# A gated mix of attention and a long convolution on one core: which operand of the convolution is turned into Toeplitz tiles

## The chip, the cores and the metric

The kernel runs on one core of a Trainium2 chip. The metric is the device time of one execution in microseconds. Engines are named as in the profile: PE (TensorE matmul), PEld (its weight load), DVE (VectorE), ACT (ScalarE), POOL (GpSimd), SP (SyncE, which issues most DMAs).

## The reference

Two branches read a 2048 x 448 bfloat16 input `x` and are mixed row by row with a gate `g = sigmoid(sum(x * gate_w))`:

```
q = x @ wq (16 heads of 28), k = x @ wk, v = x @ wv      # one k and one v for all heads
a = softmax(q k^T / sqrt(28)) v, heads joined, @ wo
K[d, l] = Re sum_n C[d,n] * dt[d]*B[d,n] * exp(dt[d]*A[d,n] * l)    # d < 448, n < 256, l < 2048
b[:, d] = causal convolution of x[:, d] with K[d, :]  +  x[:, d] * Dskip[d]
out = g * a + (1 - g) * b
```

The convolution is per channel: 448 channels, each with its own 2048 taps.

## The kernel before, in words

**One program, ordered by a planner.** The kernel first describes every piece of work as an operation with an engine, an estimated duration, what it reads and writes, and a priority. A list scheduler (`Prog.schedule`) turns this into one fixed order per engine. Each engine then runs its order strictly from front to back, waiting on semaphores where an operand comes from elsewhere. So an instruction that waits holds up everything behind it on its engine. The planner gives each DMA a fixed latency (2.2 us and an `extra`), and for some readers it adds a slack (`slk`): the first matmul on a freshly loaded convolution tile is planned 2.5 us later than its operand is expected.

**Attention** sets the pace. There are 1024 score tiles of 128 keys x 512 queries (16 groups of 4 heads x 512 queries, 64 tiles each). They are taken in sets of three and two alternately, 410 sets. For each set PE writes scores to PSUM (`psS`, line 1181), ACT takes the exponential (`expT`, line 1205), and PE multiplies by the values, accumulating in the one bank `psB` (line 1214). `psS` holds two sets; `expT` is a ring of 15 tiles. At the end of each group of 64 tiles `psB` is copied to `acc` (line 1074, by ACT for groups 0 to 13), and the next group may write `psB` only after this copy. Then a chain of three POOL DMAs turns the sums into reciprocals on all partitions (`denT`, `R_scratch`, `rdenB`). In gaps of PE the planner inserts matmuls on zeros (lines 640 and 1187), which keep PE's activity up.

**The convolution** is woven into the same orders in 14 chunks `c` of 32 channels. For each chunk:

- DVE builds tables of powers (`tables`, lines 895 to 935), from masters built for 2 to 4 chunks at a time (`masters`, lines 856 to 874).
- `kgen`: PE multiplies the tables (line 959), DVE adds `Dskip` to tap 0 (line 969), ACT copies the taps to SBUF (line 972), and POOL writes them with nine DMAs to the scratch `KP` in DRAM.
- `tload`: SP loads a Toeplitz tile for each 4 channels out of `KP`. Partition p of the tile reads the same rows shifted by one element, so that one tile is 128 partitions x 4288 elements, 1072 KB. 112 tiles are loaded, into five slots of `T` and two more that come free late.
- `conv` (two per chunk): PE multiplies the tiles by `U` (the input, loaded once in blocks of 64 rows in a reversed order, shape 128 x 32 blocks x 448 channels), line 1015; DVE multiplies by 1 - g (line 1026), PE turns the result (line 1037), and DVE adds it to `O` (line 1045).

Chunk 13 is made in two halves (`HALVES`). At the end `outp` and `tail` project the attention with `Wo` and store `O`.

Of the kernel before, what the change touches and what calls it, by code (L numbers as in the profile page):

```python
# [6 lines left out]
ALU = mybir.AluOpType  # L7
# [4 lines left out]
P = 128  # L12
# [19 lines left out]
HALVES = (13,)  # L32
NTR = 5
# [47 lines left out]
class Prog:  # L81
# [52 lines left out]
    def dma(self, pairs, desc, slot, rd=(), wr=(), pr=0, eng="sp", slow=False, extra=0):  # L134
# [5 lines left out]
        o = self.op(eng, fn, nd * (30.0 + 0.03 * size if size < 1500 else 105.0 + 0.022 * size) / 16.0 * 1.1, rd, wr, pr)  # L140
# [5 lines left out]
        return o  # L146

    def schedule(self):
# [20 lines left out]
        while done < n:  # L169
# [55 lines left out]
            if o.slot is not None:  # L225
                free[e] = r + (1000.0 if e == "pool" else 500.0) * o.ndma
                s = r if e == "pool" else max(r, dmafree)
                end = s + o.ns + self.DMA_NS + o.extra
                dmafree = max(dmafree, s) + o.ns
            else:  # L230
                free[e] = r + o.ns
                end = free[e] + o.lat
# [124 lines left out]
class Kernel:  # L357
# [34 lines left out]
    def alloc(self):  # L392
# [23 lines left out]
        self.U = sb("U", D * 32, BF)  # L416
        self.O = sb("O", 16 * D, BF)
        self.T = sb("T", NTR * TW, BF)
        self.tslots = [(self.T, s * TW, ["tpdone", "rawdone"]) for s in range(NTR)]
        self.tslots.append((self.xT, NT * S - TW - 2048, [("xT", hp, q) for hp in range(2) for q in range(3)]))  # L420
        self.tmap, self.tlast = {}, [s - 9 for s in range(NTR)] + [-20, -20]
# [14 lines left out]
        self.cst = sb("cst", 512, BF)  # L436
# [4 lines left out]
        self.KP = nc.dram_tensor("KP_scratch", (2 * KH,), BF).ap()  # L441
# [4 lines left out]
    def consts(self):  # L446
# [6 lines left out]
        dm(V(self.kstg, 0, 256), 0.0, 170, [("kst", 0, 0), ("kst", 1, 0)])  # L453
# [10 lines left out]
        for k in range(2):  # L464
            dm(V(self.U, (16 + 8 * k) * D, 8 * D), 0.0, 1550, ["Uz"])
# [17 lines left out]
        dm(V(self.Wo, 0, NT * D), 0.0, 810, ["Wo"], 5)  # L483
        for q in range(4):
            dm(V(self.O, q * 4 * D, 4 * D), 0.0, 800, [("O", q)], 5)

    def loads(self):
# [14 lines left out]
        self.dtb = self.cst  # L502
# [21 lines left out]
        rs = self.U.rs  # L524
        for k, (h, p0, b0) in enumerate(((1, 16, 15), (0, 0, 15), (1, 0, 31))):
            ap = bass.AP(tensor=self.U.h, offset=h * rs + p0 * D, ap=[[2 * rs, 64], [D, 16], [1, D]])
            pg.dma([(ap, dram(x, 64 * b0 * D, [[D, 64], [-64 * D, 16], [1, D]]))],
                   (1024, 896), f"u{k}", rd=["Uz"] if p0 else [], wr=[("U", k)], pr=0.5)
        for k in range(2, 6):
# [6 lines left out]
        pg.dma([(dram(self.KP, KH + 1024, [[4 * KW, 112], [KW, 4], [1, 64]]), self.kstg.v(0, 112, 0, [[64, 4], [1, 64]]))],  # L536
               (448, 128), "pad", rd=[("kst", 0, 0), ("kst", 1, 0)], wr=["pad"], pr=3)
# [15 lines left out]
    def prep_x(self):  # L553
# [3 lines left out]
        for q in range(4):  # L557
# [43 lines left out]
            pg.op("pe", mv, 900, rd=["Wv", "Wvg"] + self.xk(q), wr=[("b", 6)], pr=0.5)  # L601
        pg.op("dve", lambda e: e.tensor_reduce(sm.v(0, P, 12, [[1, 1]]), sm.v(0, P, 8, [[1, 4]]), AX.X, ALU.max),
# [86 lines left out]
    def prep_gate(self):  # L689
# [11 lines left out]
        def mm(e):  # L701
            for mu in range(2):
                for par in range(2):
                    r = e.matmul(px.v(0, P, 64 * mu, [[1, 64]]), self.sel.v(0, 16, 128 * (1 + (1 - mu) - par), [[1, P]]),
# [126 lines left out]
    def masters(self, b):  # L831
# [22 lines left out]
        for k in range(11):  # L854
            if k:
                dv(lambda e, k=k: e.tensor_tensor(two(msq), both(k - 1), both(k - 1), ALU.mult), 2 * w, keys(k - 1), ["msq"])  # L856
                dv(lambda e, k=k: e.scalar_tensor_tensor(src(k, 1), src(k - 1, 0), 2.0, src(k - 1, 1), ALU.mult, ALU.mult),
# [13 lines left out]
        for lv in range(5):  # L871
            if lv:
                dv(lambda e: e.tensor_tensor(qq, qq, qq, ALU.mult), w, ["sqq"], ["sqq"])
# [64 lines left out]
    def kgen(self, c, sub=None):  # L938
# [13 lines left out]
        for jj in range(8):  # L952
            def mm(e, comp, jj=jj):
                for half in range(2):
                    for g in gs:
# [7 lines left out]
                            start=(comp == 0 and half == 0), stop=(comp == 1 and half == 1),  # L963
                            tile_position=(0, 32 * g), skip_group_check=True)
                return r
            for comp in range(2):
                pg.op("pe", lambda e, mm=mm, comp=comp: mm(e, comp), 226 if whole else 113, mode="c", st=2.08 if whole else 1.04,
                      rd=keys, wr=[X] + k1 + k2, pr=1.7, lock=G if jj == 0 and comp == 0 else None)
        pg.op("dve", lambda e: e.tensor_tensor(ko.v(p0, np, ks + 63, [[64, 8]]), G.v(p0, np, 63, [[64, 8]]),
                                               self.skt.v(p0, np, 8 * c, [[1, 8]]), ALU.add),  # L970
              el(8), rd=[X, "skt"], wr=k1, pr=2)
        pg.op("act", lambda e: e.activation(ko.v(p0, np, ks, [[64, 8], [1, 63]]), G.v(p0, np, 0, [[64, 8], [1, 63]]), AF.Copy),  # L972
              490, rd=[X] + k1, wr=k2, pr=-1, unlock=G)
        rs = ko.rs
        lst = [(dram(self.KP, (32 * c + 8 * gs[0]) * KW + 1024, [[8 * KW, len(gs)], [KW, 8], [1, 64]]),
                bass.AP(tensor=ko.h, offset=(p0 + 16) * rs + ks, ap=[[32 * rs, len(gs)], [64, 8], [1, 64]]))]
        for g in gs:
            for h in range(2):
                lst.append((dram(self.KP, h * KH + (32 * c + 8 * g) * KW, [[64, 16], [KW, 8], [1, 64]]),
                            ko.v(32 * g + 16 * h, 16, ks, [[64, 8], [1, 64]])))  # L980
        pg.dma(lst, (264 * len(gs), 128), f"kw{sub or 0}", rd=k1 + k2, wr=[("KP", 2 * c + h) for h in ((0, 1) if whole else (sub,))],
               pr=0, eng="pool", extra=2000)
# [8 lines left out]
    def tload(self, gi):  # L991
# [4 lines left out]
        pg.dma([(t.v(0, P, o, [[1, TW]]),  # L996
                 dram(self.KP, 4 * gi * KW, [[1, 64], [KH, 2], [1, TW]]))],
               (128, 2 * TW), f"T{s}", rd=[("KP", gi // 4), "pad"] + x, wr=[("T", s)] + y, pr=1, extra=2500)

    def conv(self, c):  # L1000
# [3 lines left out]
        ck, cx = ("cst", c % 2), [("xT", hp, 0) for hp in range(2)] if c == 1 else []  # L1004
# [295 lines left out]
```

## Time and profile before

| | |
|---|---|
| median of 3 runs | 537.56 us (537.3 to 541.54) |
| the profiled execution's own time | 540.75 us |
| its span in the profile | 539.0 us |
| mean granted PE clock | 0.965 |
| PE busy | 486.4 us (90%) |
| DVE busy | 449.5 us (83%) |
| ACT busy | 497.5 us (92%) |
| POOL busy | 102.1 us (19%) |
| DMA | 142.89 MB, 265 GB/s on average |

Durations below come from the one profiled execution, which is 3.2 us above the median of the three runs. A group's row gives its busy time, the mean duration of one instruction, and the idle time of the engine just before it with what ended it. Durations overlap a little with the next instruction's, so where it matters the distance from start to start is used.

### The profile page before, as it was taken

The page shows a single profiled execution, that of the slowest core. Times are in us where ns is not written, and L with a number is a line of the kernel's source. Part 1 is how long each engine was busy: PE and PEld are TensorE (multiplying, and loading weights), DVE is VectorE, ACT ScalarE, POOL GpSimd, SP SyncE. Part 2 cuts the span into 40 slices and gives each one's busy share as a digit, 9 for nine tenths or more (in the row PEclk, how much of TensorE's full clock was granted, in tenths as well). Part 3 has the DMA queues.
Part 4 walks back from the last instruction along what each step waited for, and adds up shares of the span by engine and source line. Part 5 has one row for each costly group of instructions (what it writes and reads, how often), then busy time and mean ns, then how long its engine had stood idle before and what let it go on. Part 6 is the DMA issues. An engine that isn't in the chain of part 4 may idle for free.

```text
span 539.0 us, 20180 instructions
## 1 busy us (share of the span) xinstructions
PE 486.4 (90%) x9186; PEld 249.5 (46%) x9186; DVE 449.5 (83%) x891; ACT 497.5 (92%) x458; POOL 102.1 (19%) x192
## 2 busy tenths in 40 slices
PE   7698999989999899888999898989999898999887
PEld 4442233235454555353555454553556355644434
DVE  7979999989999999899999999999999695331203
ACT  3799999998999999989999999999999796899992
POOL 2000002200431404012040430040042213220000
PEclk9989999998999999999999999999999796899998
DMA  8931100793398987979778989999859997999722
GB/s 235 283 121 47 37 21 7 251 347 116 118 376 300 329 358 284 351 259 386 296 240 363 327 273 348 400 351 367 343 191 356 353 380 287 348 344 392 261 88 71
DMA packets 39042, 142.89 MB, mean 265 GB/s; under 512 B 11240, under 2 KB 22032, under 8 KB 24620
## 3 DMA queue, kind: packets, MB, share of 16 engines
q1 hardware_dynamic: 28316, 135.30, 69.0%
q0 software_dynamic: 9104, 6.13, 4.4%
q8 instruction: 72, 1.18, 0.9%
q10 hardware_dynamic: 1536, 0.17, 0.3%
q14 instruction: 14, 0.11, 0.1%
HBM read 135.39 MB, written 5.74 MB: 262 GB/s over the span
## 4 chain that ended last, share of the span: by engine, by line
ACT 56%; PE 26%; DMA 8%; DVE 8%; issue 2%; ACTq 0%
ACT expT L1205 54%; PE psS L1181 7%; PE psB L1214 4%; PE psS L959 3%; PE psX L959 3%; DMA rdenB<-R_scratch 3%; PE psX L1015 3%; DMA denT<-acc 2%; DMA sz<-in_A_wv_dram 2%; PE psS L1015 2%; ACT acc L1074 1%; DMA R_scratch<-denT 1%; DVE msq L856 1%; DVE xT L576 1%; DVE tab L911 1%
## 5 line engine op out<-in xcount | busy, mean ns | idle before, releaser
L1205 ACT ACTIVATE expT<-psS 128x1536 bf16<-128x1536 f32 (+1 forms) x410 | 470.6, 1340 | 18.7 <-PE psS L1181 11.7
L1181 PE MATMUL psS<-qT,kT 32*128 32x512 bf16 x1024 | 164.3, 395 | 29.8 <-ACT expT L1205 22.3
L1214 PE MATMUL psB<-expT,vaug 128*32 128x512 bf16 x1024 | 105.1, 400 | 3.7 <-issue 3.2
L1181 PEld LDWEIGHTS psS<-qT,kT 32*128 32x128 bf16 x1024 | 39.5, 91 | 119.3 <-ACT expT L1205 97.3
L1187 PE MATMUL psB<-ident,zero 32*128 32x512 bf16 x190 | 74.9, 394 | 0.0
L911 DVE TENSOR_TENSOR tab<-tab,mbf 128x256 bf16<-128x256 bf16 (+5 forms) x75 | 69.6, 928 | 1.2
L1015 PE MATMUL psX<-T,U 128*18 128x128 bf16 (+7 forms) x1920 | 54.7, 243 | 4.2 <-issue 3.2
L1214 PEld LDWEIGHTS psB<-expT,vaug 128*32 128x32 bf16 x1024 | 26.4, 93 | 64.8 <-issue 62.8
L1015 PEld LDWEIGHTS psX<-T,U 128*18 128x18 bf16 (+7 forms) x1920 | 47.6, 161 | 15.1 <-issue 11.2
L640 PE MATMUL psB<-ident,zero 128*32 128x512 bf16 (+3 forms) x728 | 48.6, 336 | 0.0
L138 POOL DMA_DIRECT2D KP_scratch<-xT x64 | 34.4, 544 | 43.6 <-ACT xT L972 43.6
L138 POOL DMA_DIRECT2D KP_scratch<-kstg x63 | 34.1, 549 | 34.2 <-ACT kstg L972 32.5
L959 PE MATMUL psX<-tab 128*32 128x64 bf16 x960 | 39.7, 293 | 0.3 <-DVE tab L935 0.3
L913 DVE TENSOR_TENSOR tmp<-tab,mbf 128x256 bf16<-128x256 bf16 (+4 forms) x62 | 39.6, 638 | 0.0
L1015 PE MATMUL psS<-T,U 128*32 128x128 bf16 (+7 forms) x1344 | 39.3, 243 | 0.0
L138 POOL DMA_DIRECT2D denT<-acc x15 | 10.8, 717 | 146.8 <-ACT acc L1074 137.9
L1015 PEld LDWEIGHTS psS<-T,U 128*32 128x32 bf16 (+7 forms) x1344 | 34.0, 161 | 8.9 <-issue 6.9
L959 PE MATMUL psS<-tab 128*32 128x64 bf16 x832 | 35.3, 293 | 0.0
L138 POOL DMA_DIRECT2D R_scratch<-denT x15 | 8.6, 576 | 138.7 <-DVE denT L1082 59.2
L930 DVE TENSOR_TENSOR tab<-tab,tmp 128x2048 bf16<-128x2048 bf16 x28 | 33.5, 1219 | 0.2
L959 PEld LDWEIGHTS psX<-tab 128*32 128x32 bf16 x960 | 30.3, 138 | 6.7 <-issue 3.8
L959 PEld LDWEIGHTS psS<-tab 128*32 128x32 bf16 x832 | 26.4, 137 | 7.4 <-issue 5.4
(179 smaller groups left out, 599.1 us busy)
## 6 DMA issues: line engine op xcount, KB each, us to landing
T<-KP_scratch SPq DMA_DIRECT2D x102, 1072.0 KB, 11.0
xT<-KP_scratch SPq DMA_DIRECT2D x7, 1072.0 KB, 10.5
rdenB<-R_scratch POOLq DMA_DIRECT2D x15, 256.0 KB, 12.4
tab<-KP_scratch SPq DMA_DIRECT2D x3, 1072.0 KB, 8.8
U<-in_A_x_dram SPq DMA_DIRECT2D x3, 896.0 KB, 15.4
tab<-in_A_x_dram SPq DMA_DIRECT2D x4, 448.0 KB, 7.5
SZ_scratch<-tab SPq DMA_DIRECT2D x1, 1344.0 KB, 8.6
out_dram<-O SPq DMA_DIRECT2D x3, 448.0 KB, 3.8
```

The source lines that it names most:

```text
L138: return [e.dma_start(o, i, **kw) for o, i in pairs]
L576: pg.op("dve", lambda e, d=dst, s=src: e.tensor_copy(d, s), 1130, rd=[("b", b)], wr=[key], pr=-0.6)
L640: r = e.matmul(t.v(32 * j, 32, bo, [[1, 128 * m]]), self.zero.v(0, P, 0, [[1, 32]]), self.ident.v(0, P, 0, [[0, m], [1, P]]), start=not ac ...
L911: vo(lambda e, dst=dst, src=src, mr=mr: e.tensor_tensor(dst, src, mr, ALU.mult), 2 * n, done + mk(lv), kr + ki)
L913: vo(lambda e, src=src, mi=mi, w=w, n=n, tb=tb, to=to: e.tensor_tensor(tb.v(0, P, to, [[n, 2], [cw, w], [1, cw]]), src, mi, ALU.mult), 2 * ...
L930: vo(lambda e, h=h: e.tensor_tensor(tab.v(0, P, FM + 32 * h, [[64, 2], [EW, 32], [1, 32]]), tab.v(0, P, lo + 31 * EW + 64 * h, [[BLK, 2], ...
L959: r = e.matmul(G.v(32 * g, 32, 64 * jj, [[1, 64]]), tab.v(0, P, lo + comp * BLK + 32 + o, [[EW, 32]]), tab.v(0, P, fo, [[mo - fo, 2], [EW, ...
L1015: r = e.matmul(ps.v(32 * j, 32 - 2 * n, 128 * k, [[1, 128]]), self.U.v(0, P, 2 * n * D + 4 * gi + j, [[D, 32 - 2 * n]]), tb.v(0, P, to + j ...
L1181: r = e.matmul(self.psS.v(0, P, 512 * (bo + k), [[1, 512]]), kT.v(32 * h, 32, 128 * kt, [[1, 128]]), qT.v(32 * h, 32, 512 * (i % 2), [[1, ...
L1187: r = e.matmul(self.psB.v(0, P, 0, [[1, 512]]), self.zero.v(32 * h, 32, 0, [[1, P]]), self.ident.v(32 * h, 32, 0, [[0, 4], [1, P]]), start ...
L1205: pg.op("act", lambda e: e.activation(expT.v(0, P, 512 * es, [[1, n]]), self.psS.v(0, P, 512 * bo, [[1, n]]), AF.Exp, scale=SQ), 50 + n / ...
L1214: r = e.matmul(self.psB.v(32 * h, 32, 0, [[1, 512]]), vaug.v(0, P, 32 * kt, [[1, 32]]), expT.v(0, P, 512 * (t % RING), [[1, 512]]), start= ...
```

## The change

The roles of input and taps in the convolution are exchanged.

- The Toeplitz tiles are now made of x. The transposed input `xT` is stored to a scratch `XP` in four DMAs, with a pad of zeros, and `tload` reads from there. A tile no longer depends on `kgen`. At most three tile loads are in flight (`tops`); `T` has seven slots instead of five.
- The other operand, now `Ku`, holds the taps of one chunk in two buffers. `kgen` gets them there from the ACT copy with a transposing DMA from SBUF to SBUF (`X`, issued by SP) and four POOL DMAs (from `X` to `Ku`), two of them of 64 runs of 1 KB and two of 1024 runs of 32 bytes. `U` and its three loads are gone.
- `Dskip` is added by PE: four small matmuls at the end of `kgen` instead of the DVE addition. The ACT copy moves 512 columns in one piece.
- The copies of `psB` to `acc` in groups 0 to 13 move from ACT to DVE.
- `Wo`, `Ku` and `O` are cleared by DMAs from the tile of zeros. DVE's memsets of `Wo`, `O` and `U` are gone.
- `masters` writes its last level (k = 10, lv = 4) directly in bfloat16 without a copy after it. Chunk 13 is made in one piece.
- The planner's costs for DMAs are other ones, so that all orders change. The result of the convolution comes out unreversed, and the gate's table is laid out to match.

The core of the diff:

```diff
-HALVES = (13,)
-NTR = 5
+HALVES = ()
+NTR = 7
...
-        o = self.op(eng, fn, nd * (30.0 + 0.03 * size if size < 1500 else 105.0 + 0.022 * size) / 16.0 * 1.1, rd, wr, pr)
+        o = self.op(eng, fn, nd * (12.0 + 0.036 * size if size < 1500 else 105.0 + 0.022 * size) / 16.0 * 1.1, rd, wr, pr)
...
+    def tdma(self, out, inp, slot, rd, wr, pr):
+        o = self.dma([(out, inp)], (128, 1024), slot, rd, wr, pr, extra=1500)
+        o.fn = lambda e: [e.dma_start_transpose(out, inp)]
...
-                free[e] = r + (1000.0 if e == "pool" else 500.0) * o.ndma
+                free[e] = r + (550.0 if e == "pool" else 250.0) * o.ndma
...
-        self.U = sb("U", D * 32, BF)
+        self.Ku = sb("Ku", 2 * 1024, BF)
+        self.X = sb("X", 2 * 512, BF)
...
-        for k in range(2):
-            dm(V(self.U, (16 + 8 * k) * D, 8 * D), 0.0, 1550, ["Uz"])
...
-        dm(V(self.Wo, 0, NT * D), 0.0, 810, ["Wo"], 5)
-        for q in range(4):
-            dm(V(self.O, q * 4 * D, 4 * D), 0.0, 800, [("O", q)], 5)
+        for k, (b, n, keys, pr) in enumerate(((self.Wo, 14, ["Wo"], 1.9), (self.Ku, 16, [("Ku", 0, 0), ("Ku", 0, 1), ("Ku", 1, 0), ("Ku", 1, 1)], 4),
+                                              (self.O, 56, [("O", q) for q in range(4)], 5))):
+            pg.dma([(b.v(0, P, 0, [[P, n], [1, P]]), self.zero.v(0, P, 0, [[0, n], [1, P]]))], (P * n, 256), f"z{k}", rd=["zero"], wr=keys, pr=pr)
...
+            lst = [(dram(self.XP, (q // 2) * KH + 64 + 512 * (q % 2), [[KW, DT], [DT * KW, 4], [1, 512]]),
+                    xT.v(0, DT, 2048 * q, [[512, 4], [1, 512]]))]
+            if q == 1:
+                lst.append((dram(self.XP, KH, [[KW, DT], [DT * KW, 4], [1, 64]]), xT.v(0, DT, 2048 + 448, [[512, 4], [1, 64]])))
+            pg.dma(lst, (448, 1024), "xp", rd=self.xk(q), wr=[("XP", q)], pr=0.6)
...
-        pg.op("dve", lambda e: e.tensor_tensor(ko.v(p0, np, ks + 63, [[64, 8]]), G.v(p0, np, 63, [[64, 8]]),
-                                               self.skt.v(p0, np, 8 * c, [[1, 8]]), ALU.add),
-              el(8), rd=[X, "skt"], wr=k1, pr=2)
-        pg.op("act", lambda e: e.activation(ko.v(p0, np, ks, [[64, 8], [1, 63]]), G.v(p0, np, 0, [[64, 8], [1, 63]]), AF.Copy),
-              490, rd=[X] + k1, wr=k2, pr=-1, unlock=G)
-        rs = ko.rs
-        lst = [(dram(self.KP, (32 * c + 8 * gs[0]) * KW + 1024, [[8 * KW, len(gs)], [KW, 8], [1, 64]]),
-                bass.AP(tensor=ko.h, offset=(p0 + 16) * rs + ks, ap=[[32 * rs, len(gs)], [64, 8], [1, 64]]))]
-        for g in gs:
-            for h in range(2):
-                lst.append((dram(self.KP, h * KH + (32 * c + 8 * g) * KW, [[64, 16], [KW, 8], [1, 64]]),
-                            ko.v(32 * g + 16 * h, 16, ks, [[64, 8], [1, 64]])))
+        def tap(e):
+            for g in gs:
+                r = e.matmul(G.v(32 * g, 32, 63, [[64, 8]]), self.ident.v(0, P, 32 * g, [[1, 32]]), self.skt.v(0, P, 8 * c, [[1, 8]]),
+                             start=False, stop=True, tile_position=(0, 32 * g), skip_group_check=True)
+            return r
+        pg.op("pe", tap, 113 if whole else 57, mode="c", st=0.7 if whole else 0.35, rd=["skt", "id"], wr=[X], pr=1.6)
+        pg.op("act", lambda e: e.activation(ko.v(p0, np, ks, [[1, 512]]), G.v(p0, np, 0, [[1, 512]]), AF.Copy),
+              490, rd=[X], wr=k1 + k2, pr=-1, unlock=G)
...
+        pg.tdma(self.X.v(0, P, xo + r0, [[128, 4], [1, n]]), ko.v(p0, np, ks, [[1, 512]]), f"kt{sub or 0}", rd=k1 + k2,
+                wr=xk + (["dt"] if c < 1 else []), pr=0)
+        lst = []
+        for par in range(2):
+            for h, m, w in ((0, 0, 32), (1, 16, 16)):
+                dims = [[128, 4], [1, n]] if not h else [[32, 16], [1, w]] if whole else [[128, 4], [1, w]]
+                for r in (r0,) if whole or not h else (r0, r0 + 32):
+                    lst.append((bass.AP(tensor=self.Ku.h, offset=h * rs + uo + 512 * par + r, ap=[[2 * rs, 64]] + dims),
+                                bass.AP(tensor=self.X.h, offset=64 * par * xs + xo + r + m, ap=[[xs, 64]] + dims)))
+        pg.dma(lst, (1152, 64), f"kw{sub or 0}", rd=xk, wr=[("Ku", c % 2, h) for h in hs], pr=0, eng="pool", extra=1500)
...
-        pg.dma([(t.v(0, P, o, [[1, TW]]),
-                 dram(self.KP, 4 * gi * KW, [[1, 64], [KH, 2], [1, TW]]))],
-               (128, 2 * TW), f"T{s}", rd=[("KP", gi // 4), "pad"] + x, wr=[("T", s)] + y, pr=1, extra=2500)
+        pg.dma([(t.v(0, P, o, [[1, TW]]), dram(self.XP, 4 * gi * KW + 1, [[1, 64], [KH, 2], [1, TW]]))],
+               (128, 2 * TW), f"T{s}", rd=[("XP", q) for q in range(4)] + ["pad"] + x, wr=[("T", s)] + y, pr=1, extra=1500)
+        o = pg.ops[-1]
+        self.tops.append(o.i)
+        if len(self.tops) > 3:
+            o.deps[self.tops[-4]] = 1
...
-                                     self.U.v(0, P, 2 * n * D + 4 * gi + j, [[D, 32 - 2 * n]]),
-                                     tb.v(0, P, to + j * KW + 896 - 128 * n, [[1, 128]]),
+                                     self.Ku.v(0, P, ku(4 * k + j) + 2 * n, [[1, 32 - 2 * n]]),
+                                     tb.v(0, P, to + j * KW + 128 * n, [[1, 128]]),
...
-        if i < 14:
-            pg.op("act", lambda e: e.activation(av, self.psB.v(0, P, 0, [[1, 512]]), AF.Copy), 490, rd=[("b", 6)], wr=[ak, kb], pr=-1)
-        elif i == 14:
+        if i < 15:
             pg.op("dve", lambda e: e.tensor_copy(av, self.psB.v(0, P, 0, [[1, 512]])), el(512), rd=[("b", 6)], wr=[ak, kb], pr=0)
```

## The prediction

> **What bounds the kernel now.** I read the page first: engine totals, then the chain of waits. ACT does the exponentials and is busy 92% of the span; more than half of the chain is their line.
>
> ```profile
> span 539.0 us, 20180 instructions
> ...
> PE 486.4 (90%) x9186; PEld 249.5 (46%) x9186; DVE 449.5 (83%) x891; ACT 497.5 (92%) x458; POOL 102.1 (19%) x192
> ...
> L1205 ACT ACTIVATE expT<-psS 128x1536 bf16<-128x1536 f32 (+1 forms) x410 | 470.6, 1340 | 18.7 <-PE psS L1181 11.7
> ```
>
> 410 exponentials in 470.6 us are 1.148 us for one set; this is my clock for distances below. What else lies on ACT's path? Second view: ACT's own waits between 40 us (start-up over) and 528 us (last exponential).
>
> ```profile
> ACT expT L1205 <- PE psS L1181: 9.0, 15, 1.4
> ACT expT L1205 <- PE psB L1187: 6.5, 6, 2.4
> ACT xT L972 <- DVE xT L969: 2.1, 3, 1.2
> ACT acc L1074 <- PE psB L1214: 0.2, 1, 0.2
> ```
>
> So ACT idles 17.8 us: 15.5 us for scores from PE and 2.1 us for the DVE addition ahead of the copy of the taps. The rest of ACT's path is work, in which the copies of `psB` and of the taps are the part that isn't exponentials. The timeline shows what one copy costs:
>
> ```profile
> 182.65 0.59 ACT L1074 ACTIVATE acc<-psB 128x512 f32<-128x512 f32 x1
> 183.12 1.03 ACT L1205 ACTIVATE expT<-psS 128x1024 bf16<-128x1024 f32 x1
> ```
>
> Start to start it is 0.47 us. Third view: where does PE make ACT wait? The table of stretches of 20 us (columns: PE, PEld, DVE, ACT, POOL busy, then PE clock, DMA share, GB/s):
>
> ```profile
> 400.00:420.00 20.00, 18.69 (x479) 11.63 (x476) 19.62 (x39) 20.00 (x19) 5.61 (x11) 1.00 0.80 307
> 420.00:440.00 20.00, 17.99 (x326) 9.07 (x330) 15.59 (x34) 16.57 (x16) 1.24 (x2) 0.83 0.99 361
> 440.00:460.00 20.00, 18.30 (x348) 10.74 (x352) 13.21 (x35) 15.74 (x15) 6.46 (x12) 0.71 0.85 312
> 460.00:480.00 20.00, 19.58 (x413) 12.17 (x405) 6.55 (x14) 17.70 (x18) 5.71 (x11) 0.95 1.02 349
> ```
>
> ACT loses 3.4, 4.3 and 2.3 us here, just where the granted clock is low and DMA full. The timeline shows the beginning:
>
> ```profile
> 418.33 0.39 PE L1181 MATMUL psS<-qT,kT 32*128 32x512 bf16 x3
> 421.37 0.62 PE L1214 MATMUL psB<-expT,vaug 128*32 128x512 bf16 x4 [2.65 <-issue]
> 421.77 0.54 PE L1015 MATMUL psX<-T,U 128*32 128x128 bf16 x12
> ```
>
> PE stands for 2.65 us, for nothing that the profile shows, and the conv matmuls that come next in its order wait for a tile of `T`. Loads of `T` take 9.4 to 15.9 us to land around this time. I read it as a tile that came late. ACT idles 2.36 us before its next exponential at 422.90. Smaller stalls of this kind lie at 118 to 130 us (2.1 us of ACT) and 358 to 370 us (1.7 us). With the stretch from 416 to 472 us (9.2 us) that makes 13 of ACT's 15.5 us.
>
> **What the Trainium skill says.** "TensorE: Matmul & The Clock Gate", Part 1: PE's clock is halved after a window of about 3.4 us without enough activity. The trace agrees in kind: 0.83 and 0.71 follow the stall. So one late tile costs more than its wait. "DMA: Bandwidth & Descriptors", section Queues, rings and completion order: an engine alternates between the rings of its queues by packet, and within a ring starts in order. The trace agrees: POOL's writes of 16 KB land in 1.7 us (median) from 90 to 150 us and in about 6 us beside a stream of tiles. For the change it means that a transpose, on SP's ring, stands behind the tiles already issued, up to three. Same page, Rules for kernel authors: a transpose next to ordinary DMAs needs no guard; no transpose is in this trace.
>
> **The change part by part**, against the profiled 540.75 us (span 539.0 and 1.75 around it).
>
> 1. *Copies of `psB` off ACT.* 14 x 0.48 = -6.7 us. "ScalarE: Activation LUTs", What ACT_TABLE_LOAD costs, prices an ACTIVATE of 512 columns at 186 + 427 ns less 93 ns of overlap, 0.52 us, so the size fits.
> 2. *Taps.* 15 copies become 14: -0.5. The DVE addition ahead of them goes: -2.1, ACT's measured wait. In its place PE does four matmuls of 8 columns, 56 in all; a matmul of 64 columns in the same tiling comes every 30 ns or so, hence 0.12 us a chunk, which I cost at nothing, since PE leads ACT by up to two sets there.
> 3. *Start.* Two of the 0.81 us memsets of `O` stand on the chain at 16.5 and 22.5 us, where DVE sets the time. Up to -1.6; the next things there are PE and ACT steps, so I take -1. The clearing DMAs (11,008 runs of 256 bytes, 2.8 MB) take the place of `U`'s 2.75 MB.
> 4. *Tiles no longer behind `kgen`.* Today the tile of a chunk can be asked for only after the taps are in DRAM, with five slots. Afterwards only slots and the limit of three hold it back. The 112 tiles are 120,000 KB of the 142.89 MB; at 376 GB/s, the fastest full stretch, 2.9 us each, 328 us in all, and the window for them begins some 35 us earlier than 97.5 us. Gain between 0 and the 13 us of stalls. PE also gets weights in neighbouring columns; loads with a stride last 161 ns on average (line 1015), neighbouring ones 93 ns (line 1214), but they overlap matmuls, so I give that nothing. I take -5 for the part: tiles are still loaded at close to full DMA in the later half.
> 5. *`Ku` comes late instead.* This is the added wait: the first conv matmul of a chunk waits for copy, transpose and four POOL DMAs, and behind it on PE stand the next scores, for which ACT waits. In the order built for the changed kernel I count the score sets between the tap matmuls of a chunk and its first conv matmul: 12, 11.2, 18.8, 19.2, 16, 14.8, 21.2, 16, 15.2, 10.8, 14.8, 14.8, 22, 14. Times 1.148 us that is 12.4 us at the least, 13.8 and 12.9 next, 16 us or more otherwise. What must fit: copy 1.8 us (one set until its turn, 0.6 itself); transpose: below, the 1.7 us that the quickest DMA here takes to land; above, 4 x 1309 ns ("VectorE: DVE Perf Modes", The three transpose paths, a 128 x 128 block) plus 1.7 plus three tiles ahead, some 15 us; I take 5. POOL's issue: today 5.01 us for nine DMAs, 0.56 each. Two of the four now have 1024 runs. If issue doesn't grow with runs 0.55 us, if it grows in proportion from 128 runs eight times that, 4.4 us; I take 1, so 3.1 us for four. Landing 1.7 to 6.3 us, I take 5. Sum 15 us. Three chunks miss by 1.2, 2.1 and 2.6 us; PE's lead of about one set takes 1.1 us off each: +2.5 us. With 12 us it is 0; with 22 us +48.
> 6. *Copies of `psB` on DVE.* 14 x 0.69 = 9.7 us more DVE work, against memsets (7.3 us), tap additions (15 x 0.19), copies in `masters` (about 2.6) and the double pass for chunk 13: DVE does not become the bound by its sum. But the next group's first values matmul waits for this copy, and DVE may be inside an operation of up to 2.29 us. Between a group's last and next group's first values matmul lie 0.8 to 2 sets, and ACT has one more in hand. Between 0 and 1 us each; I take 0.1: +1.5.
> 7. *POOL and SP.* 101 DMAs instead of 172 on POOL; its chain for the reciprocals has 28 us between groups. Nothing.
>
> Sum: 540.75 - 6.7 - 0.5 - 2.1 - 1 - 5 + 2.5 + 1.5 = 529.4 us profiled. The median of the runs lies 3.2 below the profiled execution: 526 us.
>
> **Rivals.**
>
> - *A, slower: `Ku` late.* If the way from tap to `Ku` is 20 us and not 15, ten chunks miss, by 39.8 us together, 28 us after PE's lead. 526 - 2.5 + 28 = 551 us. For it: a transpose on the ring of the tiles, and 1024 runs a DMA that POOL may have to write out one by one. Against it: nine POOL DMAs and their landing took 6.3 us together at 91 us. It cancels the gain from about 18 us on (12 us lost).
> - *B, no change: DVE late for `psB`.* 14 copies that each cost ACT 1 us give 526 + 12.5 = 538.5 us. For it: DVE is at 19 of 20 us through most of the span. Against it: the planner knows the wait and places the copy.
> - *C, tile stalls stay.* DMA is as full as before, the late half as loaded. Then step 4 is 0: 531 us.
>
> **How the numbers follow.** Forecast 0.46, C 0.18, B 0.11, A 0.25. Forecast and C are faster by over 1% (below 532.2 us; 1% is about what a measurement of this kernel can tell from no change), B is the same, A slower. Predicted 526 us. The forecast's own range is 518 (all of the 13 us gained) to 533. To leave no more than 2 in 10 out, the range reaches to A's 551: 518 to 551.
>
> **What would show it.** Right: ACT's row keeps 410 exponentials and loses line 1074's 14 copies; ACT's wait for the DVE addition is gone; PE's clock shows no 0.71 stretch; tile loads begin near 60 us. Step 5 right: PE stands at most 1 to 3 us before the first conv matmul of chunks 0, 1 and 9, and at no others. Wrong: transposes that land after more than 6 us, POOL issues of over 2 us for `Ku<-X`, PE idle before conv in most chunks (A), or PE idle before line 1236's first matmul of a group, released by DVE's `acc` (B). A time above 533 us makes the forecast wrong.

## The result, and the profile after

The changed kernel takes 569.45 us (median of four runs, 566.6 to 571.82); the kernel before, measured on the same chip, 537.43 us. The ratio is 1.058, 95% interval 1.050 to 1.066: slower by 32 us, where the prediction said 526 us. Later runs stand beside their own runs of the kernel before, so they are compared by ratio; 1% is 5.4 us. Executions in a slower state, some per cent longer, are left out of the ratios, which leaves only two of the kernel before beside a1 to a4, and these four intervals are wide.

The page of the changed kernel: busy time, PE's granted clock, DMA's share and rate in 40 slices, ends of the chain, and the row of the exponentials.

```profile
span 570.1 us, 20425 instructions
...
PE 495.5 (87%) x9318; PEld 229.3 (40%) x9333; DVE 446.3 (78%) x845; ACT 493.3 (87%) x443; POOL 71.9 (13%) x121
...
PEclk9759999989999897999899988799678998797798
...
ACT 37%; PE 27%; DMA 21%; DVE 8%; issue 4%; POOL 2%; ACTq 0%
...
L1227 ACT ACTIVATE expT<-psS 128x1536 bf16<-128x1536 f32 (+1 forms) x410 | 471.8, 1305 | 53.3 <-PE psS L1203 44.4
```

The exponentials take as long as before (471.8 us against 470.6), and ACT's work as a whole fell by 4.2 us. What grew is the idle time just before them: 53.3 us, where it was 18.7. These 34.6 us are the whole 31 us of the span and a little more. In the chain, ACT's share fell from 56% to 37% and DMA's rose from 8% to 21%, and PE's granted clock is lower in many slices (0.907 on average, 0.965 before), as it was around single stalls before. ACT's waits between 40 and 560 us say for whom, and PE's own waits say where PE lost time (the columns: total us, times, longest):

```profile
ACT expT L1227 <- PE psS L1203: 43.3, 33, 4.4
ACT expT L1227 <- PE psB L1209: 7.5, 8, 3.0
```

```profile
PE psS L1203 <- ACT expT L1227: 14.5, 44, 1.7
PE psX L1039 <- issue: 9.7, 6, 3.7
PE psS L1039 <- issue: 8.4, 5, 3.3
PE psX L1039 <- DMA Ku<-X: 7.0, 2, 4.0
PE psB L1236 <- DVE acc L1098: 3.6, 2, 2.8
...
PE psX L1061 <- DVE xT L1050: 3.2, 1, 3.2
PE psS L1061 <- DVE xT L1050: 1.8, 1, 1.8
```

The wait for `Ku` that the prediction was about is there, but it is 7.0 us in two places. The wait for DVE's copy of `psB` is 3.6 us. The larger share, 18.1 us, stands before convolution matmuls (line 1039) with nothing but "issue" against it. The kernel before has such waits too, 6.4 us in two rows:

```profile
PE psX L1015 <- issue: 3.2, 3, 1.7
PE psB L1214 <- issue: 3.2, 2, 2.6
```

The timeline of PE around one of the changed kernel's shows the form: the values are multiplied at 491.00, then nothing, then the convolution goes on in the middle of its tiles.

```profile
491.00 0.40 PE L1236 MATMUL psB<-expT,vaug 128*32 128x512 bf16 x4
494.90 0.40 PE L1039 MATMUL psX<-T,Ku 128*28 128x128 bf16 x8 [3.50 <-issue]
```

The prediction read the large stall of this kind as a tile that came late. The traces say otherwise. No row of PE's list, in either kernel, has PE waiting for a tile of `T`. PE's instructions themselves come by DMA, on a queue of their own:

```profile
q8 instruction: 73, 1.20, 0.9%
```

A packet is 16 KB, and there is one for each 256 instructions of PE (in the kernel before 72 packets for some 18,400 matmuls and weight loads). Its four "issue" waits of over 1 us, the one at 421.37 among them, all end 1.3 to 1.5 us after such a packet has ended, and all stand at the same place, number 194, of a block of 256. In the changed kernel seven of eight end 1.2 to 1.6 us after a packet (the place can't be counted there, since 15 of PE's records are missing); the packet before 494.90 began at 488.98 and ended at 493.27, where others take about 1.07 us. So PE stood for its next instructions, which share the DMA engines with everything else. This rests on times and places; no run moves the instructions alone.

In which state is DMA meanwhile? The stretches from 300 to 400 us (columns: PE, PEld, DVE, ACT, POOL busy, PE clock, DMA share, GB/s), first of the kernel before, then of the changed one:

```profile
300.00:400.00 100.00, 91.33 (x1859) 48.14 (x1853) 97.08 (x188) 97.65 (x91) 24.18 (x42) 0.98 0.93 337
```

```profile
300.00:400.00 100.00, 88.72 (x1788) 41.53 (x1788) 89.94 (x176) 90.38 (x81) 16.48 (x25) 0.92 0.98 307
```

DMA engines are fuller and carry 9% less. That should make a reader suspicious: something occupies them that brings few bytes.

### The profile page after: what moved, and what is told of

Its sections match the earlier page's. It is cut to its first block, busy times and chain, and to the rows that moved or that the text cites. A ratio compares the mean times of both kernels' runs of the same rounds, so it can differ in the third digit from the quotient of the medians.

```text
span 570.1 us, 20425 instructions
## 1 busy us (share of the span) xinstructions
PE 495.5 (87%) x9318; PEld 229.3 (40%) x9333; DVE 446.3 (78%) x845; ACT 493.3 (87%) x443; POOL 71.9 (13%) x121
## 3 DMA queue, kind: packets, MB, share of 16 engines
q1 hardware_dynamic: 46188, 139.09, 76.1%
## 4 chain that ended last, share of the span: by engine, by line
ACT 37%; PE 27%; DMA 21%; DVE 8%; issue 4%; POOL 2%; ACTq 0%
ACT expT L1227 36%; DMA rdenB<-R_scratch 11%; PE psS L1203 8%; PE psB L1236 5%; PE psX L1039 3%; DMA Ku<-X 3%; DMA X<-xT 3%; DMA R_scratch<-denT 2%; DMA sz<-in_gate_w_dram 2%; PE psS L1039 2%; POOL Ku L138 2%; PE psS L971 1%; PE psX L971 1%; DMA X<-kstg 1%; DVE tab L923 1%
## 5 line engine op out<-in xcount | busy, mean ns | idle before, releaser
L1227 ACT ACTIVATE expT<-psS 128x1536 bf16<-128x1536 f32 (+1 forms) x410 | 471.8, 1305 | 53.3 <-PE psS L1203 44.4
L923 DVE TENSOR_TENSOR tab<-tab,mbf 128x256 bf16<-128x256 bf16 (+4 forms) x70 | 68.5, 980 | 0.9
L1039 PE MATMUL psX<-T,Ku 128*18 128x128 bf16 (+7 forms) x1856 | 47.0, 237 | 16.8 <-issue 9.7
L1039 PEld LDWEIGHTS psX<-T,Ku 128*18 128x18 bf16 (+7 forms) x1856 | 34.6, 101 | 31.8 <-issue 20.4
L138 POOL DMA_DIRECT2D Ku<-X x56 | 38.5, 697 | 47.5 <-DMA X<-kstg 30.0
L1039 PE MATMUL psS<-T,Ku 128*32 128x128 bf16 (+4 forms) x1504 | 37.5, 236 | 7.1 <-issue 6.3
L925 DVE TENSOR_TENSOR tmp<-tab,mbf 128x256 bf16<-128x256 bf16 (+3 forms) x56 | 36.3, 647 | 0.0
L1039 PEld LDWEIGHTS psS<-T,Ku 128*32 128x32 bf16 (+4 forms) x1504 | 27.4, 100 | 19.2 <-issue 15.3
L925 DVE TENSOR_TENSOR tab<-tab,mbf 128x4096 bf16<-128x4096 bf16 x14 | 31.8, 2271 | 3.3 <-PE psX L971 2.6
L1050 DVE TENSOR_TENSOR xT<-psX,omq 128x512 bf16<-128x512 f32 x15 | 10.2, 681 | 30.0 <-PE psX L1039 30.0
L642 PEld LDWEIGHTS psB<-ident,zero 128*32 128x32 bf16 x836 | 19.7, 97 | 17.1 <-issue 8.8
```

The source lines that it names most:

```text
L138: return [e.dma_start(o, i, **kw) for o, i in pairs]
L642: r = e.matmul(t.v(32 * j, 32, bo, [[1, 128 * m]]), self.zero.v(0, P, 0, [[1, 32]]), self.ident.v(0, P, 0, [[0, m], [1, P]]), start=not ac ...
L923: vo(lambda e, dst=dst, src=src, mr=mr: e.tensor_tensor(dst, src, mr, ALU.mult), 2 * n, done + mk(lv), kr + ki)
L925: vo(lambda e, src=src, mi=mi, w=w, n=n, tb=tb, to=to: e.tensor_tensor(tb.v(0, P, to, [[n, 2], [cw, w], [1, cw]]), src, mi, ALU.mult), 2 * ...
L1039: r = e.matmul(ps.v(32 * j, 32 - 2 * n, 128 * k, [[1, 128]]), self.Ku.v(0, P, ku(4 * k + j) + 2 * n, [[1, 32 - 2 * n]]), tb.v(0, P, to + j ...
L1050: pg.op("dve", lambda e: e.tensor_tensor(cb.v(0, P, co, [[128, 4], [64, 2], [1, 64]]), ps.v(0, P, 0, [[128, 4], [64, 2], [1, 64]]), self.o ...
```

## The experiments

Theories before the first run: K, `Ku` comes late; T, the tiles of `T` come late behind the limit of three and behind waiting transposes; D, the copies of `psB` on DVE. Edits are shown against the changed kernel unless another is named; where it is said that the order is kept, the planner sees the same operations and only what a DMA moves is different.

**a1, transfers into `Ku` small (`small` is a copy of 64 bytes, from the third chunk on), order kept.**

```diff
-        o.fn = lambda e: [e.dma_start_transpose(out, inp)]
+        o.fn = lambda e: [e.dma_start(*small) if small else e.dma_start_transpose(out, inp)]
...
+        if c > 1:
+            lst = [(self.Ku.v(k, 1, uo, [[1, 32]]), self.X.v(0, 1, xo + r0, [[1, 32]])) for k in range(len(lst))]
```

> The changed kernel with its order kept; from the third chunk on the transpose and the four POOL DMAs into Ku move 64 bytes each, so Ku holds old data (part of the result is left out). Issues, waits and semaphores stay. If the lateness of Ku costs the time (theory K), most of the 32 us over the kernel before go: 540 to 550 us. If the late thing is the tiles of T behind the limit of three and behind waiting transposes (theory T), Ku's own weight is the 8 us in which PE stood for it in chunks 5, 9 and 11: 560 to 564 us. If the copies of psB on DVE cost it (theory D), no change: 567 to 572 us.

Measured: ratio 0.999, 0.979 to 1.020 (538.33 us). Nearly the whole loss is gone, more than theory T or D allows; the interval leaves about 2% either way.

**a2, tiles small, order kept.** From the second use of its slot on, a tile moves 128 bytes in place of 1072 KB.

```diff
+        if s in self.tseen:
+            o.fn = lambda e: [e.dma_start(t.v(0, 1, o_, [[1, 64]]), dram(self.XP, 4 * gi * KW + 1, [[1, 1], [1, 64]]))]
```

> The changed kernel with its order kept; each tile of T after the first use of its slot moves 128 bytes, so conv multiplies by old tiles (part of the result is left out). Theory T: the late tiles are gone, and the DMA load with them: 540 to 550 us. Theory K: PE still stands for Ku, 558 to 566 us, less what the transposes gain by standing behind nothing. Theory D: 565 to 572 us.

Measured: 0.957, 0.945 to 0.970 (513.73 us). With `Ku`'s transfers in full and the tiles gone, nothing is late, PE's instructions neither: there is no "issue" wait of over 1 us. ACT's waits from 40 us on are down to

```profile
ACT O L1180 <- PE psS L1167: 5.4, 2, 4.6
ACT expT L1232 <- PE psS L1208: 0.7, 1, 0.7
```

of which the first is the end of the kernel.

**a3, both small.**

> Both together: what is left over the prediction of 526 us is neither transfer time of Ku nor of T. Theories T and K: 525 to 535 us. Theory D: above 550 us.

Measured: 0.959, 0.947 to 0.971 (514.55 us), no different from a2. So `Ku`'s transfers cost 31 us beside the tiles and nothing without them. Theory D is out as the cause of the loss, since DVE's copies are the same in all three.

**a4, copies of `psB` back on ACT, planned anew** (`if i < 14:` with the old `activation`).

> The changed kernel with the first 14 copies of psB back on ACT, as before; the order is planned anew. Theory D: DVE waits go and 6.7 us of ACT work come, 550 to 558 us. Theories T and K: the copies only add ACT work, 569 to 577 us.

Measured: 1.079, 1.061 to 1.096, against 1.058 (1.050 to 1.066). The copies on DVE are not what costs. That the change would be slower still without them isn't shown: the intervals touch, and the order is another one.

So it is `Ku`'s transfers together with the tiles. That leaves two readings: they are late because tiles stand ahead of them (K), or the load that they put on the DMA engines holds other transfers up (call it M).

**b2, `Ku` in full, but nobody waits for it; order kept.** `late` holds the POOL DMAs of chunks 2 to 13.

```diff
-                    lst.append((bass.AP(tensor=self.Ku.h, offset=h * rs + uo + 512 * par + r, ap=[[2 * rs, 64]] + dims),
+                    lst.append((bass.AP(tensor=(self.Kd if c > 1 else self.Ku).h, offset=h * rs + uo + 512 * par + r, ap=[[2 * rs, 64]] + dims),
...
             self.pg.schedule()
+            for o in self.pg.ops:
+                if o.eng == "pe":
+                    for d in self.late & set(o.deps):
+                        del o.deps[d]
```

> The changed kernel with its order, transposes and POOL DMAs kept in full, but from the third chunk on the POOL DMAs write to a buffer that nobody reads, and conv doesn't wait for them (it reads the Ku of the first two chunks, so part of the result is left out). If Ku costs by coming late (theory K): as with Ku's transfers small, 535 to 545 us. If it costs by the load that transposes and 32-byte runs put on the DMA engines and by SP's place for the transposes (theory M): little gain, 560 to 570 us.

Measured: 1.051, 1.045 to 1.057 (563.14 us). This run decides between the two readings. All the transfers, no wait for them: still slower by 5.1%. No transfers, all the waits (a1): no loss. The wait for `Ku` is worth 1.058 - 1.051 = 0.7%, 3.5 us, which the two intervals don't tell from nothing; the load is worth 1.051 - 0.999 = 5.2%, 28 us, of which a1's interval leaves about 11 us open either way (c1 and c2 below, the waits included, come to 5.1% together). ACT's waits in b2 are hardly shorter than in the changed kernel, and PE now has the tile in its list under its own name:

```profile
ACT expT L1235 <- PE psS L1211: 35.3, 32, 4.1
```

```profile
PE psX L1047 <- issue: 12.4, 7, 3.8
...
PE psX L1047 <- DMA T<-XP_scratch: 3.8, 3, 2.1
```

What does the load do to the tiles? I took from the traces the landing times of tiles that follow each other, where the later one had been issued at least 2.5 us before the earlier one landed, so that the stream was running (97 of the 112 landings are in the changed kernel's trace). With neither transpose nor `Ku` DMA under way between them they are some 2.8 us apart (median of 47), with `Ku` DMAs alone 4.10 us (20); in a1, with the small `Ku` DMAs, 2.78 (25). For the transposes the same sorting proves nothing: it gives 3.72 us (18), but also 3.43 (21) in a1, where 12 of the 14 are copies of 64 bytes. Gaps in which a transpose lands are 3.76 us (7), 4.44 in b2 (8) and 3.12 in a1 (7), so about 1 us, from few cases. An example from the changed kernel: landings at 489.92 and 492.63 (2.71 apart), then a transpose lands at 494.56 and the next tile at 497.66 (5.03), then `Ku`'s DMAs, tiles at 502.46 and 506.00 (4.80, 3.54), then 508.66 (2.66). In the table of stretches, 480 to 500 us, changed kernel and a1:

```profile
480.00:500.00 20.00, 15.63 (x363) 7.96 (x356) 14.73 (x20) 15.09 (x14) 3.43 (x5) 0.77 1.07 284
```

```profile
480.00:500.00 20.00, 15.71 (x437) 9.02 (x433) 2.09 (x4) 18.00 (x17) 3.28 (x6) 1.00 1.02 355
```

Both are full; with the transfers into `Ku` 284 GB/s get through, without them 355.

And how does the load reach PE? Not by more of "issue": a1 has nearly as much of it as the changed kernel (15.6 us against 18.1) and no loss.

```profile
PE psS L1041 <- issue: 8.4, 5, 2.4
PE psX L1041 <- issue: 7.2, 6, 2.3
```

Late instructions are a price of the tile stream, which both have. Against a1, whose page says

```profile
span 536.1 us, 20440 instructions
...
PE 478.2 (89%) x9333; PEld 221.0 (41%) x9333; DVE 445.5 (83%) x845; ACT 489.8 (91%) x443; POOL 62.7 (12%) x121
```

PE of the changed kernel is idle for 16.7 us more (74.6 against 57.9) and busy for 17.3 us more with the same instructions: the clock is at half for 107 us of its trace (from 492.5 and from 519.8 us, for instance, in the stalls that begin at 491.4 and 518.1), for 42 of a1's. Of the idle time 7.0 us are the wait for `Ku`, 5.0 us (line 1061) and 2.0 us more (line 1236) waits for DVE. Two of the changed kernel's waits for DVE, of 3.2 and 2.8 us, go back to a DMA that the theories leave out, that of the reciprocals `rdenB`: DVE stands for it for 4.1 us until 187.4 and for 2.8 us until 218.3, and what comes next in its order is late for PE at 196 and 220. DVE's waits for it, before and changed:

```profile
DVE onT L1088 <- DMA rdenB<-R_scratch: 2.2, 2, 1.5
```

```profile
DVE onT L1110 <- DMA rdenB<-R_scratch: 10.6, 4, 4.1
```

They are 6.9 us in a1, 0.3 in a2 and 20.1 in b2, where PE is idle for as long as in the changed kernel (75.1 us) without any wait for `Ku`. So the load reaches PE through small transfers that come late, in one place or another, and through the clock that falls with the stalls. No run separates these ways.

**c1, POOL DMAs small, transposes in full; c2, the reverse; order kept.**

> The changed kernel with its order and its transposes kept in full; from the third chunk on only the four POOL DMAs into Ku move 64 bytes each (part of the result is left out). If it is the POOL DMAs that hold up the tile stream (theory N; two tiles that land one after the other are 4.1 us apart when a Ku DMA lies between them and 2.8 without): 542 to 550 us, a ratio of 1.01 to 1.025. If the transposes hold it up (theory X; 3.7 us apart with a transpose between them): 556 to 564 us, 1.035 to 1.05.

> The counterpart: POOL DMAs into Ku in full, the transposes from the third chunk on move 64 bytes (part of the result is left out). Theory N: 556 to 564 us, a ratio of 1.035 to 1.05. Theory X: 542 to 550 us, 1.01 to 1.025. If both transfers share the cost by halves, both kernels come to about 1.03.

Measured: c1 1.029 (1.022 to 1.037), c2 1.035 (1.026 to 1.044). Taking the POOL DMAs away brings 2.9%, taking the transposes away 2.3%, together 5.1% of the 5.9% of a1. Each is about half, as far as intervals of 0.7 to 0.9% either way tell; neither theory N nor X is right alone.

**c3, long runs in the POOL DMAs, order kept.**

```diff
-                dims = [[128, 4], [1, n]] if not h else [[32, 16], [1, w]] if whole else [[128, 4], [1, w]]
+                dims = [[1, 496]] if h and c > 1 else [[128, 4], [1, n]] if not h else [[32, 16], [1, w]] if whole else [[128, 4], [1, w]]
```

> The changed kernel with its order and all transfers; from the third chunk on the two POOL DMAs that write 16 columns of every 32 (1024 runs of 32 bytes each) write 496 columns in a row instead (64 runs of 992 bytes; the columns that must stay zero aren't, so the result differs). If the short runs are what costs (theory N with runs as its cause): like the kernel with small Ku DMAs. If it is their bytes or their number of DMAs: no change, a ratio of 1.055 to 1.06.

Measured: 1.035 (1.026 to 1.044). More bytes in longer runs bring 2.3% of c1's 2.9%. Most of the POOL DMAs' cost is that of the two with 1024 runs of 32 bytes, 32 KB each, and lies in the runs and not in what they carry.

**b1, six tiles in flight in place of three, planned anew.**

> The changed kernel with up to six tile loads in flight in place of three; the order is planned anew. If the limit of three starves conv (theory L: each load takes some 9.6 us to land, so three in flight give at best one tile per 3.2 us): 545 to 558 us, and SP's 173 us of waiting for a tile's landing mostly gone. If the tile stream is costly because transposes and Ku's DMAs stand behind tiles in the rings (theory R): more tiles ahead of them, 570 to 590 us.

Measured: 1.060 (1.054 to 1.066). No change; a tile now takes 13.6 us to land (median) instead of 9.6. The limit of three is not the cause, which fits a PE that waits for no tile.

**b3, planner told later landings** (`extra` of transposes 5500, `Ku` 4500, tiles 4500, each 1500 before).

> The changed kernel with the planner told latencies closer to the measured ones: transposes 4 us, Ku's DMAs 3 us and tiles 3 us later than it assumed; only the order changes. If the loss is an order built too tightly for what the transfers take (theory P): 540 to 555 us. If there is no room to place conv later, or DMA itself is the bound (theory L): 562 to 580 us.

Measured: 1.043 (1.037 to 1.049). A quarter of the loss. An order that expects the real latencies hides some of it; the time lies between the two ranges, so the order has a share and is not the cause.

**d1, the kernel before with small tiles, order kept** (the edit of a2).

> The kernel before with its order kept; each tile of T after the first use of its slot moves 128 bytes (part of the result is left out). The same edit of the changed kernel took 513.7 us, a ratio of 0.957. If the prediction's savings on ACT's path are real and only the tile stream takes them back (6.7 + 0.5 + 2.1 + 1 = 10.3 us): 521 to 526 us, a ratio near 0.975. If they are not there: 511 to 516 us, 0.957. The prediction put the late tiles at 13 of ACT's 15.5 us here: 523 us.

Measured: 0.972 (0.966 to 0.977; 521.92 us). So the transfers of the tiles cost the kernel before 2.8%, 15 us, and the changed kernel without tiles is faster than the kernel before without tiles by 0.9715 - 0.9572 = 1.4%, 7.7 us (both intervals together leave about 7 us either way).

```profile
ACT O L1157 <- PE psS L1144: 5.5, 2, 4.1
ACT expT L1209 <- PE psS L1185: 2.7, 4, 1.5
```

**b4, the kernel before with the 14 copies of `psB` on DVE, planned anew.**

> The kernel before with only the first 14 copies of psB moved from ACT to DVE (one part of the change alone); the order is planned anew. By the prediction's steps 1 and 6: -6.7 + 1.5 = -5.2 us, a ratio of 0.990. If ACT was held by late tiles and the tiles take the gain back (theory T): a ratio of 0.995 to 1.005. If DVE's lateness for psB costs more than it brings (theory D): above 1.005.

Measured: 1.026 (1.018 to 1.034). ACT's path did get shorter: the last exponential ends at 513.7 us of the trace, against 527.7 before. But the last convolution matmul ends at 530.0 instead of 517.9, three stalls of about 2 us just ahead of it, two for the last tiles and one that ends 1.5 us after a packet of instructions, and ACT stands at the end:

```profile
ACT O L1151 <- PE psS L1138: 22.5, 2, 22.3
ACT expT L1203 <- PE psS L1179: 9.3, 11, 2.2
```

The kernel has two chains that end at about the same time. Time taken off ACT counts only as far as the convolution keeps up. Why the convolution came later in this order isn't settled: the order was planned anew, and no run separates DVE's extra work from it.

**e1 to e4, transposes on PE.** To take `Ku`'s DMAs out of a kernel that computes everything, PE transposes the taps (matmuls with the identity, and with one shifted by 16 rows), DVE copies them into `Ku`, and the partitions of a tile lie with the two halves of x one below the other. e2 has later tiles in the plan, e4 five in flight, e3 both.

```diff
-                 dram(self.XP, 4 * gi * KW + 1, [[1, 64], [KH, 2], [1, TW]]))],
+                 dram(self.XP, 4 * gi * KW + 1, [[KH, 2], [1, 64], [1, TW]]))],
```

> The changed kernel without any DMA into Ku: 16 matmuls of 128 columns with the identity (and with one whose rows are shifted by 16) transpose the taps on PE, two copies of 512 columns on DVE bring them into Ku, and tiles of T lie with their two halves one below the other. If the 31 us are the load of those DMAs on the tile stream (theory M): as with Ku's transfers small, 0.995 to 1.01 of the kernel before, 533 to 543 us, less whatever 14 x 1.2 us more on DVE cost. If DVE's copies take the gain back (theory D): 1.02 to 1.04.

> The kernel with PE's transposes, and the planner told that a tile takes 3 us longer to land; only the order changes. What is left of late tiles (some 24 us with Ku's transfers small, against 15 in the kernel before) is an order built for faster tiles (theory P): faster than with PE's transposes alone by 1 to 2%. If it is the limit of three or DMA itself: within 0.5% of it.

> PE's transposes, the later tiles in the plan and five loads in flight together. Theories P and L both: 2 to 3% faster than PE's transposes alone, and the fastest kernel here, 0.97 to 0.985 of the kernel before. Neither: no change.

> PE's transposes with up to five loads in flight in place of three, the plan's tile latency as in the changed kernel. If the limit of three starves conv once the Ku DMAs are gone (theory L): 1 to 2% faster than PE's transposes alone. If not: within 0.5% of it, as six in flight made no difference with the Ku DMAs in place.

Measured: 2409, 2410, 2417 and 2410 us, 4.5 times the kernel before. e1's page and PE's waits:

```profile
HBM read 132.64 MB, written 5.74 MB: 57 GB/s over the span
```

```profile
PE psX L1045 <- DMA T<-XP_scratch: 907.8, 53, 20.1
PE psS L1045 <- DMA T<-XP_scratch: 686.7, 41, 19.8
```

PE waits some 20 us for each tile. The Trainium skill, "DMA: Bandwidth & Descriptors", Rules for kernel authors, says that an outermost dimension of fewer than 16 entries confines the whole DMA to at most that many engines; the new order has 2 outermost. The trace agrees: e1's queue moves its 137.25 MB with 14.5% of 16 engines' time, 2.3 engines on average. The four runs say nothing on the question they were made for.

**f1 and f2, the same as e1 and e3 with two DMAs of 64 partitions for a tile.**

```diff
+        pg.dma([(t.v(64 * h, 64, o, [[1, TW]]), dram(self.XP, h * KH + 4 * gi * KW + 1, [[1, 64], [1, TW]])) for h in range(2)],
```

> PE's transposes as in the run before, but each tile of T by two DMAs of 64 partitions in place of one whose first dimension has two entries (which took 20 us a tile). Theory M (the 31 us were the load of transposes and POOL DMAs): 0.995 to 1.01 of the kernel before, 533 to 543 us. If DVE's 28 more copies of 512 columns or the doubled number of SP's issues take the gain back: 1.02 to 1.04. If the landing of a tile is still above 15 us: far slower.

> The same, with the planner told that a tile takes 3 us longer and with five loads in flight. If what is left of late tiles comes from the order and the limit (theories P and L): 1.5 to 3% faster than without these two edits, 0.97 to 0.99 of the kernel before. If the tile stream itself is the bound, as it was with six in flight: within 0.7% of it.

Measured: 1.334 (1.327 to 1.341) and 1.314 (1.306 to 1.321). f1's queue and issues:

```profile
q1 hardware_dynamic: 40364, 137.26, 87.6%
...
T<-XP_scratch SPq DMA_DIRECT2D x210, 536.0 KB, 13.3
```

87.6% of 16 engines for 715.5 us is 627 us for 137 MB; in the changed kernel it is 76.1% of 570.1, 434 us for 139 MB. Half tiles land 2.64 us apart, so the stream runs at about 208 GB/s. A transfer of half the partitions goes at little more than half the rate. Whether that comes from SBUF's side (64 partitions) or from DRAM's (all rows from one half of `XP`) isn't separated by these runs. So a whole kernel without `Ku`'s DMAs and with tiles at full rate was not found, and no version measured here that does all the work beats the kernel before.

## Why the prediction was wrong

The failing step is 5, and not in its sum but in its question. It asked how long the way to `Ku` is and whether the first convolution matmul must wait for it. That part came near: transposes and POOL DMAs of the changed kernel,

```profile
L150 SPq DMA_TRANSPOSE X<-kstg x7: 1189/1215/2222, 95.7 to 484.1; - x7
L150 SPq DMA_TRANSPOSE X<-xT x7: 1190/1238/2109, 133.6 to 516.1; - x7
...
DMA to landing us min/median/max: 2.9/6.1/10.6
```

```profile
L138 POOL DMA_DIRECT2D Ku<-X x56: 529/694/873, 99.3 to 529.2; - x56
...
DMA to landing us min/median/max: 1.9/6.7/9.2
```

The transpose took 6.1 us where 5 was assumed, POOL's issue four times 0.7 = 2.8 us where 3.1 was, the landing 6.7 us where 5 was, and from the copy to the last landing it was 8.4 to 24.5 us by chunk, in eleven of fourteen more than the 15 of the sum. The wait itself costs 0.7%, 3.5 us (b2), near the +2.5, with luck: the way was longer than assumed, and two chunks waited. What the step left out is the other direction. It said that a transpose stands behind the tiles in SP's ring; it didn't ask what then stands behind the transposes. Fourteen transposes and 56 POOL DMAs, of which half are made of 32-byte runs, were given a latency and no occupancy, so what they take from other transfers stood in the sum at nothing. It costs 28 us, with about 11 us left open either way.

- *Steps 1, 2, 3 and 6*: summed, they gave -8.8 us. With the tile stream out of the way the two kernels differ by 7.7 us (a2 against d1), which agrees, with about 7 us of uncertainty. The copies on ACT and the wait for the DVE addition are gone from the profile. Alone in the kernel before, steps 1 and 6 give +2.6% (b4) and not -1%: the gain was on ACT's chain, and the end went over to the convolution. The start brought nothing: the first exponential begins at 28.0 us against 26.7.
- *Step 4*, tiles no longer behind `kgen`, -5: wrong. The first tile is asked for at 65.3 us instead of 97.5, as expected, but no gain is seen. The reading of the kernel before that it rests on came out in its size and not in its mechanism: the stalls were put at 13 us of late tiles, and without the tiles' transfers the kernel before gains 15 (d1). But PE waited for no tile there; the stalls at 360, 419 and 447 us are late instructions, and those from 118 to 130 us are waits for DVE (lines 822 and 828). The agreement is luck: small tiles free the DMA engines for the instructions too. Removing `Ku`'s transfers leaves 0.999 - 0.957 = 4.2%, 23 us, as the cost of the tiles' transfers in the changed kernel; the interval of a1 doesn't say whether that is more than before. An earlier start of the first load does nothing against it.
- *Step 7*, POOL and SP at nothing: POOL's issues are no trouble, but its chain for the reciprocals, which was to have 28 us of room, holds DVE up for 10.6 us where it was 2.2. On SP, a transpose that waits for ACT's copy holds the tiles behind it, up to 16.3 us at a time. In a1 these waits are as long, and the loss is gone, so it is not the main cause; its own share wasn't measured.
- *Rivals.* A said 551 us by a way to `Ku` of 20 us. The direction is right and the mechanism isn't: b2 takes the wait away and the loss stays. B, DVE late for `psB`, is 3.6 us of PE's waits, and 2.8 of them come from `rdenB`. C had the stalls stay; what the tiles' transfers cost grew from 15 to 54 us (1.058 - 0.957), since the new transfers go through the same engines.
- *What would show it.* One sign listed for A, transposes landing after more than 6 us, did come; POOL issues of over 2 us did not (0.87 at most). PE waited for `Ku` in chunks 5 and 9, 4.0 and 3.0 us, where chunks 0, 1 and 9 were named. PE's clock, expected to lose its 0.71 stretch, has 0.77 from 480 to 500 us.

## What to carry to other kernels

Price a DMA twice: once by its latency for whoever waits for it, and once by what it takes from engines that are already near full, which its bytes don't tell. Small runs and transposes are paid by the neighbours, the fetching of instructions and small transfers on other chains among them, so look at DMA share beside GB/s: fuller engines that carry less say that something else occupies them. A wait for "issue" is no proof of a late operand: look where in the instruction stream it stands, and what the instruction queue did. And an engine relieved of work gives its time back only if the other chain, here the convolution, can end earlier too.

## What the runs showed of the hardware

- PE's instructions come by DMA, 16 KB for each 256. Where such a packet is late, PE stands until 1.2 to 1.6 us after its end, and the profile names no releaser ("issue"): four waits of over 1 us in the kernel before, seven in the changed one, eight in a1, none in a2 and d1, where the tiles are small.
- Four POOL DMAs from SBUF to SBUF, two of them with 1024 runs of 32 bytes, set a running stream of 1072 KB tiles back by about 1.3 us per tile in whose time they fall (4.10 against 2.78 us in a1); a transpose of 128 x 512 bfloat16 by about 1 us, from few cases. Without the stream the POOL DMAs of 64 KB land in 2.2 us (a2), beside it in 6.5.
- POOL's issue of a DMA takes 0.54 us with 64 runs and 0.85 with 1024; SP's issue of a transpose 1.2 us, where that of a tile is 0.5 us.
- The order of the two outer dimensions of a tile, 64 x 2 or 2 x 64, decides between some 3 and 20 us a tile; two DMAs of 64 partitions take together nearly twice as long as one of 128.
- Six loads in flight move no more than three: landing went from 9.6 to 13.6 us.
